# Moving loads to GpSimd's queue, building a v block on chip, storing in row pairs and doubling the output buffers, in a dilated sliding-window attention kernel with a gated output

## The chip, the cores and the metric

The kernel runs on one core of a Trainium2 chip. The metric is the device time of one execution in microseconds (us). A core has TensorE (PE in the profile; its weight loads are PEld), VectorE (DVE), ScalarE (ACT), GpSimd (POOL) and SyncE (SP), and 16 DMA engines that carry every transfer between device memory and the on-chip memory, whichever engine issued it. Each execution is given a state, fast or slow. It is slow when it took over 1.5% longer than the fastest of the same kernel.

## The reference

q, k and v have the shape (8 batches, 8 heads, 576 positions, 64). Heads 0 to 3 attend to the last 32 positions ("plain" heads). Heads 4 to 7 attend to every fourth position of the last 128 ("dilated" heads). The result x (8, 576, 512) goes through a gated unit:

```python
mask_plain = (rel >= 0) & (rel < 32)
mask_dil = (rel >= 0) & (rel < 128) & (rel % 4 == 0)
...                       # softmax, times v, heads joined to x
for k in range(5):
    gate_pre += conv_w[k] * xp[:, k:k + S, :]      # causal convolution in time
gate = 1 / (1 + exp(-gate_pre))
out = (gate * (x @ w_val)) @ w_out
```

## The kernel before

A batch has four pairs of heads: two plain, two dilated. The program walks over the 32 pairs in one hand-made order. For each pair TensorE makes scores, ScalarE the exponentials, VectorE the mask; TensorE multiplies by v, and then come the convolution, the product with w_val and, a batch later, the output tiles (w_out). In a dilated head the 576 positions are four residues of 144. The first 128 of each residue are a block of their own (vA). The last 16 of each, with the keys they need, are gathered in a second block (vB). TensorE works on two halves of the output; the second uses copies of the weights with their head halves swapped (w_val_s, w_out_s), which GpSimd makes on chip.

The parts that the change touches:

```python
out_pool = ctx.enter_context(tc.tile_pool(name="osb", bufs=4))
...
def load_v(g, a=0, e=4, eng=nc.sync):          # group g = batch, plain or dilated
    if not dil:
        for z in range(2):
            load_v_half(g, z, a, e, eng)       # plain: 64 partitions, runs of 512 bytes
    else:
        eng.dma_start(out=t["vst"][:, a:e, :], in_=v[...rows 0:512...])
        eng.dma_start(out=t["vBst"][:, a:e]..., in_=v[...rows 320:576...])
def load_group(g):                             # all on SP's queue, in this order
    k, q, remainder of k, remainder of q, then load_v(g)
def prep_v(i):                                 # GpSimd: float32 to bf16
    plain:   vP <- vPst
    dilated: vA <- vst ; vB <- vBst
def swap_out(h, m):                            # GpSimd, eight calls at pair 6
    nc.gpsimd.tensor_copy(w_out_s[D*h:D*h+D, m, :], w_st[1][D-D*h:2*D-D*h, m, :])
def out_tile(G, n):
    ...                                        # four matmuls
    osb = out_pool.tile([128, Dm], FP32, name="osb")
    nc.scalar.mul(out=osb, in_=ps, mul=0.5)
    ...
    nc.sync.dma_start(out=out[b].rearrange("(t r) n -> r t n", r=4)[r, t:t + w, :],
                      in_=osb[p:p + w, :])     # rows of one residue only
```

The softmax here doesn't subtract the row's maximum and nothing guards it: scores larger than these inputs give would overflow.

## Time and profile before

| | before |
|---|---|
| time, median of 3 (range) | 179.03 us (178.08 to 181.53) |
| span of the profiled run, state | 176.8 us, fast |
| PE busy | 159.5 us, 90% |
| bytes moved by DMA | 43.43 MB |
| longest hole of PE after 20 us | 1.33 us |

The prediction below shows and reads the main lines. The page's list of DMA queues (packets, MB, share of 16 engines' span):

```profile
q1 hardware_dynamic: 50944, 42.67, 89.1%
```

And the loads of the small remainders of q and k (qk_rest), issue to landing:

```profile
DMA to landing us min/median/max: 3.6/5.9/9.4
```

Nearly all bytes go through one queue, SP's, in packets of 42.67 MB / 50944 = 0.84 KB, and no remainder takes over 9.4 us. In this trace the transfers of that queue also land in the order of their issue: all 155 whose landing is recorded do.

### The profile page before, as it was taken

The numbers are of one execution on the slowest core, as the hardware profiler recorded it, in microseconds if no ns is written. First come the engines' busy times: TensorE is split into PE (matmuls) and PEld (weight loads), VectorE is DVE, ScalarE is ACT, GpSimd is POOL, SyncE is SP. The second block draws the span as 40 slices with busy tenths as digits, with TensorE's granted clock in tenths as the row PEclk, the third lists the DMA queues.
The fourth block names the chain that finished last, engine by engine and source line by source line (L and its number), as shares of the span: only waits on it lengthen the run. The fifth ranks groups of instructions, "written<-read, shape, count | busy, mean of one in ns | idle before, by whom it ended". The sixth has DMA issues, their size and how long they took to land.

```text
span 176.8 us, 6900 instructions
## 1 busy us (share of the span) xinstructions
PE 159.5 (90%) x2875; PEld 106.6 (60%) x2875; DVE 119.5 (68%) x299; ACT 113.8 (64%) x215; POOL 64.5 (36%) x129
## 2 busy tenths in 40 slices
PE   6798877989898899999997999789999999999990
PEld 2355544666576676677665667557677766665540
DVE  4397849773768776888695677577697869783320
ACT  3437835558777577778776777378867886654441
POOL 7673449659407610770085009300940500000000
PEclk9969999999999999999999999999999999999998
DMA  4999999999999999999999999999999322224344
GB/s 148 240 268 348 325 230 285 324 303 237 296 335 243 318 335 343 173 287 356 307 188 300 345 318 192 330 323 329 204 360 339 112 63 59 63 63 120 102 159 155
DMA packets 51528, 43.43 MB, mean 246 GB/s; under 512 B 6965, under 2 KB 45861, under 8 KB 51498
## 3 DMA queue, kind: packets, MB, share of 16 engines
q1 hardware_dynamic: 50944, 42.67, 89.1%
q8 instruction: 22, 0.36, 0.9%
q10 hardware_dynamic: 554, 0.34, 0.6%
q14 instruction: 8, 0.07, 0.1%
HBM read 33.56 MB, written 9.44 MB: 243 GB/s over the span
## 4 chain that ended last, share of the span: by engine, by line
PE 63%; DMA 21%; ACT 6%; DVE 5%; issue 2%; SPq 1%; ACTq 0%
PE ps_bank L628 16%; PE ps_bank L611 15%; PE ps_bank L594 10%; DMA out_dram<-osb 8%; PE ps_bank L378 5%; DMA qk_rest<-in_q_dram 4%; DMA k_nat<-in_k_dram 3%; DMA vPst<-in_v_dram 3%; PE ps_sc L499 3%; PE ps_sc L513 3%; PE ps_sc L449 3%; PE ps_bank L548 2%; DMA q_nat<-in_q_dram 2%; PE ps_sc L466 2%; DVE et L478 2%
## 5 line engine op out<-in xcount | busy, mean ns | idle before, releaser
L469 ACT ACTIVATE et<-ps_sc 128x576 bf16<-128x576 f32 x64 | 38.2, 649 | 13.7 <-PE ps_sc L449 9.0
L633 ACT ACTIVATE osb<-ps_bank 128x512 f32<-128x512 f32 x36 | 21.9, 609 | 28.9 <-PE ps_bank L628 18.0
L617 DVE SCALAR_TENSOR_TENSOR y<-gate,ps_bank 128x288 bf16<-128x288 bf16 x64 | 28.3, 450 | 13.0 <-PE ps_bank L611 10.6
L594 PE MATMUL ps_bank<-xT,conv_diag 64*64 64x288 bf16 (+1 forms) x768 | 27.6, 266 | 0.6 <-ACT osb L633 0.6
L529 DVE TENSOR_TENSOR xn<-ps_sc,rec 128x768 bf16<-128x768 f32 (+1 forms) x27 | 25.8, 955 | 0.9
L603 ACT ACTIVATE gate<-ps_bank 128x288 bf16<-128x288 f32 x64 | 23.1, 423 | 1.8 <-PE ps_bank L594 1.7
L478 DVE TENSOR_TENSOR et<-et,mask_d 128x576 bf16<-128x576 bf16 x32 | 15.8, 495 | 10.2 <-ACT et L469 10.2
L611 PE MATMUL ps_bank<-xT,w_val_s 128*128 128x288 bf16 x128 | 20.7, 285 | 2.1 <-issue 1.3
L193 POOL CAST k_b<-k_nat 128x512 bf16<-128x512 f32 x10 | 6.5, 681 | 42.3 <-DMA k_nat<-in_k_dram 33.1
L594 PEld LDWEIGHTS <-conv_diag 64*64 64x64 bf16 x768 | 18.9, 106 | 3.6 <-issue 1.2
L611 PE MATMUL ps_bank<-xT,w_val_b 128*128 128x288 bf16 x128 | 20.1, 286 | 0.4 <-DVE xT L563 0.4
L628 PEld LDWEIGHTS <-y 128*128 128x128 bf16 x144 | 12.6, 97 | 11.8 <-DVE y L617 0.9
L478 DVE TENSOR_TENSOR et<-et,mask_p 128x576 bf16<-128x576 bf16 x32 | 16.0, 501 | 4.8 <-ACT et L469 4.8
L202 POOL CAST vP<-vPst 128x768 bf16<-128x768 f32 x16 | 13.1, 841 | 15.6 <-DMA vPst<-in_v_dram 5.8
L628 PE MATMUL ps_bank<-w_out_s,y 128*128 128x512 bf16 x72 | 18.3, 379 | 0.1
L628 PE MATMUL ps_bank<-w_out_b,y 128*128 128x512 bf16 x72 | 18.5, 379 | 0.0
L563 DVE COPY xT<-ps_bank 128x576 bf16<-128x576 bf16 x32 | 14.6, 455 | 4.7 <-PE ps_bank L561 2.4
L611 PEld LDWEIGHTS <-w_val_s 128*128 128x128 bf16 x128 | 12.0, 97 | 6.2 <-issue 1.0
L207 POOL CAST vA<-v_st 128x512 bf16<-128x512 f32 x16 | 11.3, 705 | 10.3 <-DMA v_st<-in_v_dram 5.3
L611 PEld LDWEIGHTS <-w_val_b 128*128 128x128 bf16 x128 | 11.6, 98 | 3.7 <-issue 0.2
L393 ACT COPY kT<-ps_bank 128x1024 bf16<-128x1024 bf16 (+1 forms) x10 | 8.5, 849 | 6.1 <-PE ps_bank L370 5.9
L528 DVE RECIPROCAL rec<-ps_sc 128x12 f32<-128x12 f32 (+1 forms) x27 | 6.2, 231 | 7.7 <-PE ps_sc L499 6.7
(100 smaller groups left out, 248.4 us busy)
## 6 DMA issues: line engine op xcount, KB each, us to landing
k_nat<-in_k_dram SPq DMA_DIRECT2D x12, 512.0 KB, 6.0
q_nat<-in_q_dram SPq DMA_DIRECT2D x12, 512.0 KB, 6.9
vPst<-in_v_dram SPq DMA_DIRECT2D x12, 384.0 KB, 7.7
v_st<-in_v_dram SPq DMA_DIRECT2D x6, 512.0 KB, 5.7
k_nat<-in_k_dram SPq DMA_DIRECT2D x8, 256.0 KB, 5.9
out_dram<-osb SPq DMA_DIRECT2D x8, 256.0 KB, 6.1
q_nat<-in_q_dram SPq DMA_DIRECT2D x7, 256.0 KB, 5.8
out_dram<-osb SPq DMA_DIRECT2D x8, 224.0 KB, 5.4
```

What stands on the lines that cost most here:

```text
L202: nc.gpsimd.tensor_copy(vPs[b % NVP][:, a:e, :, 0:D], vPst[b % NVP][:, a * NB // 2:e * NB // 2, :].rearrange("p (h u) (j d) -> p h (u j) d ...
L207: nc.gpsimd.tensor_copy(vAs[b % NVD][:, a:e, :, 0:D], t["vst"][:, a:e, :].rearrange("p h (r d) -> p h r d", r=DIL))
L469: nc.scalar.activation(out=e3, in_=ps[:, :, 0:HB], func=AF.Exp, scale=scale)
L478: nc.vector.tensor_tensor(out=e3, in0=e3, in1=m, op=ALU.mult)
L529: nc.vector.tensor_tensor(out=dst, in0=av[:, :, :, 0:D], in1=rec[0:R, :, :, None].to_broadcast([R, 2, 6, D]), op=ALU.mult)
L563: nc.vector.tensor_copy(xTs[b % NXT][:, c, :, 2:], pr)
L594: nc.tensor.matmul(out=pss[G][D * hp:D * hp + D, o * T:(o + n) * T], lhsT=conv_diag[D * h:D * h + D, c, K - 1 - m, :], rhs=xt[D * h:D * h ...
L603: nc.scalar.activation(out=gate, in_=pss[G][:, 0:HB], func=AF.Tanh, scale=0.5)
L611: nc.tensor.matmul(out=ps[:, 0:HB], lhsT=w[:, mc, c * 128:(c + 1) * 128], rhs=xt[:, mc, 2 * G:2 * G + 2, 2:], start=(mc == 0), stop=(mc == ...
L617: nc.vector.scalar_tensor_tensor(out=y_half[G][:, c, b % YB * HB:(b % YB + 1) * HB], in0=gates.pop((b, c, G)), scalar=1.0, in1=ps[:, 0:HB] ...
L628: nc.tensor.matmul(out=ps, lhsT=y_half[G][:, c, y0:y0 + 128], rhs=w[:, c, :], start=(c == 0), stop=(c == NCH - 1),)
L633: nc.scalar.mul(out=osb, in_=ps, mul=0.5)
```

## The change

Its intent is to take work from the full DMA engines and from SP. It has four parts: the first rows of vB are copied on chip from vA's staging tile, so that only 64 KB per batch are loaded for it; the plain v of batches 2 to 7 and the small remainders of dilated v are issued by GpSimd instead of SP; the output rows are stored in row pairs, with 48 stores instead of 64; and there are eight output buffers instead of four. The diff, cut to its core (the constant mask and key layout for vB change with it):

```diff
-    out_pool = ctx.enter_context(tc.tile_pool(name="osb", bufs=4))
+    out_pool = ctx.enter_context(tc.tile_pool(name="osb", bufs=8))
...                                                       # load_v, dilated
-            eng.dma_start(out=t["vBst"]..., in_=v[b, 4 + a:4 + e, DIL * TB:S, :]...)
+            for w in range(2):
+                eng.dma_start(out=t["vR"][D * w + 32:D * w + 32 + TR, a:e, :], in_=...)
...                                                       # load_group
-        load_v(g)
+        if g % 2:
+            load_v(g, 0, 4, nc.gpsimd)
...                                                       # prep_v, dilated
-            nc.gpsimd.tensor_copy(vBs[...][:, a:e, :, 0:D], t["vBst"][:, a:e, :, :])
+            for w in range(2):
+                for (p0, n, src) in ((0, 32, t["vst"][96:128, ...]), (32, 16, t["vR"][...])):
+                    nc.gpsimd.tensor_copy(vBs[...][D*w+p0:D*w+p0+n, a:e, :, 0:D], src...)
...                                                       # out_tile
-                out=out[b].rearrange("(t r) n -> r t n", r=4)[r, t:t + w, :],
+                out=bass.AP(..., ap=[[DIL * Dm, w // 2], [Dm, 2], [1, Dm]]),
...                                                       # main loop
         elif i == 5:
             prep_v(7)
+            load_v(4, 0, 4, nc.gpsimd)                    # plain v of batches 2 and 3:
+            load_v(6, 0, 4, nc.gpsimd)                    # four transfers
         elif i == 6:
             ...swap_out(h, m)...                          # w_out_s
         elif i > 6:
+            if c == 0 and b + 2 < B:
+                load_v(2 * (b + 2), 0, 4, nc.gpsimd)      # batches 4 to 7: eight transfers
```

## The prediction

> **What bounds the kernel now.** I read the page's busy shares first, then the table of stretches, the chain that ended last, the list of waits, and last the timelines of single engines where a gap stood out.
>
> ```profile
> PE 159.5 (90%) x2875; PEld 106.6 (60%) x2875; DVE 119.5 (68%) x299; ACT 113.8 (64%) x215; POOL 64.5 (36%) x129
> DMA  4999999999999999999999999999999322224344
> 20.00:30.00 10.00, 7.56 (x169) 4.82 (x165) 7.18 (x21) 4.91 (x11) 6.19 (x13) 1.00 1.13 248
> 90.00:100.00 10.00, 8.69 (x151) 5.73 (x152) 6.46 (x16) 6.12 (x11) 5.11 (x9) 1.00 1.08 282
> 110.00:120.00 10.00, 8.49 (x141) 5.64 (x142) 6.42 (x16) 5.83 (x11) 1.80 (x3) 1.00 1.06 326
> 140.00:150.00 10.00, 10.00 (x204) 6.75 (x203) 7.84 (x19) 7.17 (x14) 0.00 (x0) 1.00 0.19 55
> ```
>
> The first two lines are from the page, the rest from the table of stretches (after the length: PE, weight loads, DVE, ACT, POOL, then granted clock, DMA share, GB/s). The DMA engines are full until about 137 us, yet that is not the bound for most of it: from 40 us on PE is busy 9.4 to 10 of each 10 us, and it stays so after 140 us, when the DMA share is only 0.19. The exceptions are the start (7.56 at 20 to 30 us), 90 to 100 us and 110 to 120 us. So there are two stages: a start fed by DMA, then a long stage at PE's pace with a few holes.
>
> The size of the holes follows from the chain. The same instruction (the transposes of line 378, second pair of a batch) marks the batches:
>
> ```profile
> 72.06 0.45 PE ps_bank L378 x8
> ...
> 89.68 0.45 PE ps_bank L378 x8
> ...
> 94.91 1.31 issue
> ...
> 107.40 6.62 DMA out_dram<-osb
> ...
> 129.95 0.45 PE ps_bank L378 x8
> ...
> 147.57 0.45 PE ps_bank L378 x8
> ```
>
> A batch takes 89.68 - 72.06 = 17.62 us with four output tiles, and again 147.57 - 129.95 = 17.62. The two between take 40.27. They hold one output tile more each (0.87 us of PE in the chain), so 2 x 17.62 + 2 x 0.87 = 36.98 was due, and 3.3 us are lost. The 1.31 "issue" is one part of it; the other, 2.0 us, is the store that the chain passes through:
>
> ```profile
> ACT osb L633 <- DMA out_dram<-osb: 5.7, 3, 2.8
> PE ps_bank L611 <- issue: 1.3, 1, 1.3
> ```
>
> With four output buffers, ACT's eviction waits until a store issued four tiles before has landed (here 6.6 us under full queues); ACT being in order, the exponentials behind it start late and PE with them. The first of the three such waits (1.75 us at 61.3 us) cost PE 0.56.
>
> **What the Trainium skill says.** "DMA: Bandwidth & Descriptors", section "Issuing engines are not separate DMA queues": transfers from every issuing engine share the same 16 DMA engines, so another queue saves only issue time. I therefore count nothing for bandwidth in moving plain v to GpSimd; the trace of before has no GpSimd transfer and cannot confirm it. The same page, section "SWDGE vs HWDGE vs iDMA": a transfer issued from GpSimd has its descriptors computed by the Q7 cores. So GpSimd pays for it in its own instruction stream, at a price this trace doesn't show. "GPSIMD Engine Reference", section "Specifications": each core owns 16 partitions. A copy over 16 or 32 partitions should thus cost what its length in a partition costs. The trace agrees: casts of 512 elements take 610 ns on 64 partitions (w_out_s) and 631 on 128 (w_out_b).
>
> **The change, part by part.**
>
> Second dilated v block. Before, it is read whole from memory:
>
> ```profile
> vB_st<-in_v_dram SPq DMA_DIRECT2D x6, 256.0 KB, 6.1
> vB_st<-in_v_dram SPq DMA_DIRECT2D x4, 128.0 KB, 5.2
> ```
>
> That is 2,048 KB. Now only the 16 last rows of each residue come from memory: 64 KB per batch, 512 KB in all; 1.5 MB of 43.4 MB go away. On the path this counts only in the start. There, PE waits 1.33 us for k of pair 4 (22.6 us) and then for its q. Two of these blocks are queued before it, 192 KB less; at the 330 GB/s of that stretch this is 0.6 us. The price is on GpSimd: one cast (0.40 us for 256 elements) becomes four of the same length, about 1.2 us more per pair, or, where the heads are now taken four at a time, four of 0.62 instead of two of 0.41. ACT's kB copy shrinks from 384 to 256 columns (0.53 to about 0.4 us, six times), off the path. DVE gets four memsets more of some 0.5 us, but it idles 2.38 us before its first real work at 5.73 us: nothing.
>
> Eight output buffers. A store may now land eight tiles later, some 30 us at a tile every 4.4 us, against landings of 2 to 8.5 us. All three waits should go: 2.0 us at 105 to 116 us and 0.56 us at 61 us, say 2.4 us.
>
> Row pairs. 64 stores become 48 and the bytes stay. The issues (0.42 us each) are on SP, which is off the path. DVE's line 617 writes every second element, but reads float32 from PSUM at 450 ns for 288 elements, about one element a cycle already; I count no change. PE's instructions are the same, in the same order.
>
> Plain v on GpSimd's queue. 24 transfers move there (12 plain, 12 remainders). SP loses waits and issues, off the path. But four of them, the plain v of batches 2 and 3, are put just before the swapped copy of w_out, and that copy has a deadline:
>
> ```profile
> 38.69 0.63 POOL L210 CAST vB<-vB_st 128x256 bf16<-128x256 f32 x1
> 39.38 5.24 POOL L355 CAST w_out_s<-w_st 64x512 bf16<-64x512 f32 x8
> ...
> 46.03 1.02 PE L628 MATMUL ps_bank<-w_out_s,y 128*128 128x512 bf16 x4
> ```
>
> The copy ends at 44.62 and PE reads it at 46.03: 1.4 us of slack. Afterwards pair 7's v lands some 0.9 us sooner (288 KB less in front of it), its three more casts take up to 1.2 us, and PE arrives about 0.6 us earlier. That leaves 1.4 + 0.9 - 1.2 - 0.6 = 0.5 us of slack for four issues. SP needs 0.65 us for one such transfer of plain v (1.31 for two), each of 768 runs of 512 bytes; a software generator is hardly faster. At 0.65 us the four take 2.6 and PE stalls 2.1 us; at 1 us each 3.5; at 0.3 each under 1. I choose 2.2 us, below the middle, since the small casts could overlap on different cores and the place looks chosen. A stall here is paid in full, for PE has no idle time left afterwards.
>
> Dilated v in batch 2. The vB cast ended at 56.5 us and PE needed it at 58.76. Behind the same cast of k it now ends after 1.0 + 4 x 0.62 = 3.5 us instead of 1.0; 0.3 us may be lost. Later batches had 3.7 us of slack or more.
>
> The "issue" hole of 1.31 us stands where nothing visible waited. If it is an instruction fetch delayed by full DMA queues, fewer bytes may remove it: I take half, 0.65.
>
> Sum: -0.6 - 2.4 - 0.65 + 2.2 + 0.3 = -1.15 us. From the median of 179.0 that is about 177.8; I shade it to 177.5 because the stall is the least certain term and the only large one against the change.
>
> **The rivals.** (1) GpSimd takes the place of the store wait: issues of 1.5 us and more push the swapped weights 5 us or more past PE's need, and the time becomes 180 to 182. For it: 1.4 us of slack, and an in-order engine. Against it: GpSimd is busy only 36%, and the issue cost is unknown. (2) Issues are almost free, and the smaller load of the queues removes the 1.31 us hole too: -0.6 - 2.4 - 1.3 makes 174.7. For it: the plain 3.3 us in the chain. (3) Full queues: GpSimd's ring gets its turns on the same engines, so q and k land later and the start gains nothing, while stores have their buffers: about 177. Against it: the total of bytes falls. (4) All of it hidden: PE's work is unchanged, its idle time from 46 us to 172 us is only about 4.8 us, so more than 6 us of gain, start included, is not there.
>
> **Range and chances.** The two ends are rivals 2 and 1: 174.0 to 181.0 should hold it 8 times in 10. Faster by over 2% means below 175.4, which needs nearly the whole of the gains and a stall under half a microsecond: 0.23. Slower by over 2% means above 182.6, which needs issues near 2 us: 0.06. The rest, 0.71, lies within 2%.
>
> **What would show it.** In the changed kernel's waits, ACT's eviction should not wait for stores any more, and the batches should come every 17.6 us, or 18.5 with five tiles. In GpSimd's timeline the swapped copy should start 2 to 4 us after the last vB cast of pair 7, and PE should show an idle stretch of about 2 us before the first tile of the swapped weights, near 46 us. k of pair 4 should arrive about 0.6 us earlier. The prediction is wrong if GpSimd's issues cost well under 0.4 or over 1.5 us, if DVE's strided write is slower than 450 ns, or if new waits for v on GpSimd's queue appear in later batches.

## The result, and the profile after

The changed kernel took 189.73 us (median of four, 187.53 to 191.85; the kernel before, now with four runs, 180.28 in the same rounds). A ratio here is the mean time of one kernel's fast runs over that of the other's of the same rounds, so it isn't quite the ratio of the medians. It was 1.0515, 95% interval 1.0444 to 1.0586: slower. The changed kernel was run once more as an experiment ("after2" below, on another chip): 187.99 us, ratio 1.037 (1.0287 to 1.0452). The loss is 4 to 5%.

The first profile after fell in the slow state (span 190.1), so I read the second, which is fast (span 185.6). The page of the second, busy shares, DMA slices and queues:

```profile
PE 161.3 (87%) x2875; PEld 107.5 (58%) x2875; DVE 123.0 (66%) x301; ACT 113.8 (61%) x215; POOL 93.0 (50%) x166
DMA  5997999789999999999999999979487122122244
...
q1 hardware_dynamic: 37408, 35.98, 67.1%
q0 software_dynamic: 1728, 5.11, 12.9%
```

PE's busy time is 1.8 us longer (161.3 against 159.5 us), so 7.0 of the 8.8 us of span are idle time of PE. GpSimd's own queue has appeared (q0), and its packets are of another size: 5.11 MB / 1728 = 2.96 KB against 35.98 MB / 37408 = 0.96 KB on SP's queue. In engine time a packet of q0 takes 12.9% x 16 x 185.6 / 1728 = 0.22 us, one of q1 0.053 us.

The table of stretches of the same run (columns as in the prediction):

```profile
20.00:30.00 10.00, 6.87 (x130) 4.49 (x123) 4.73 (x14) 4.80 (x10) 5.75 (x12) 0.83 1.14 261
44.00:56.00 12.00, 8.31 (x162) 4.99 (x162) 4.15 (x11) 8.21 (x16) 8.64 (x13) 1.00 1.09 253
90.00:100.00 10.00, 8.52 (x180) 5.77 (x177) 7.21 (x16) 6.70 (x14) 7.88 (x11) 1.00 1.04 244
110.00:120.00 10.00, 8.26 (x176) 5.55 (x175) 6.70 (x15) 6.21 (x12) 5.32 (x9) 1.00 1.02 305
```

The stretch from 44 to 56 us, where the kernel before has PE busy for 11.42 of the 12 us, now has 8.31. GpSimd's and PE's timelines show what happens there and later (start, us, engine, line, operation; in brackets the idle time before it and what ended it):

```profile
42.78 3.00 POOL L156 DMA_DIRECT2D vPst<-in_v_dram  x4
45.83 5.48 POOL L360 CAST w_out_s<-w_st 64x512 bf16<-64x512 f32 x8
54.27 1.46 POOL L209 CAST vP<-vPst 128x1536 bf16<-128x1536 f32 x1 [2.96 <-DMA vPst<-in_v_dram]
60.27 1.17 POOL L197 CAST k_b<-k_nat 128x512 bf16<-128x512 f32 x2 [2.06 <-DMA k_nat<-in_k_dram]
```

```profile
50.03 0.38 PE L633 MATMUL ps_bank<-w_out_s,y 128*128 128x512 bf16 x1 [0.95 <-POOL w_out_s L360]
51.36 0.38 PE L633 MATMUL ps_bank<-w_out_s,y 128*128 128x512 bf16 x1 [0.95 <-POOL w_out_s L360]
55.79 0.55 PE L501 MATMUL ps_sc<-vP,et 64*128 64x65 bf16 x24 [0.96 <-POOL vP L209]
...
97.93 0.20 PE L451 MATMUL ps_sc<-qT,kT 64*64 64x96 bf16 x1 [1.48 <-issue]
114.16 0.78 PE L596 MATMUL ps_bank<-xT,conv_diag 64*64 64x288 bf16 x21 [1.74 <-issue]
```

An issue costs GpSimd 0.75 us (four in 3.00). The eight copies of w_out_s come behind them and PE waits for them. GpSimd itself then idles for v and for k. Later PE stops twice for "issue", that is, for nothing that the profile shows. The loads on SP's queue explain the late k. The landing times of the remainders, then two of their issues in SP's timeline:

```profile
DMA to landing us min/median/max: 3.8/6.6/19.6
```

```profile
45.03 6.01 SPq L136 DMA_DIRECT2D qk_rest<-in_k_dram  x1
51.10 0.62 SPq L136 DMA_DIRECT2D qk_rest<-in_q_dram  x1
```

The longest landing is 19.6 us (9.4 before; 22.4 in the slow profile). SP was held for 6.01 us in the first issue, where the next takes 0.62. k itself took up to 16.6 us (8.4 before).

One part of the prediction came true in the main. ScalarE's evictions waited for a store twice, for 1.0 us in all, instead of three times and 5.7 us. Their list of waits is now headed by a wait for PE, which is a consequence, not a cause:

```profile
ACT osb L638 <- PE ps_bank L633: 26.8, 25, 3.5
```

### The profile page after: what moved, and what is told of

It is laid out like the page before. It is cut to its first block, busy times and chain, and to the rows that moved or that the text cites. A ratio compares the mean times of both kernels' runs of the same rounds, so it can differ in the third digit from the quotient of the medians.

```text
span 190.1 us, 6884 instructions
## 1 busy us (share of the span) xinstructions
PE 166.1 (87%) x2875; PEld 109.6 (58%) x2875; DVE 124.3 (65%) x301; ACT 113.9 (60%) x215; POOL 93.4 (49%) x166
## 2 busy tenths in 40 slices
DMA packets 39722, 41.87 MB, mean 220 GB/s; under 512 B 6870, under 2 KB 32710, under 8 KB 39691
## 3 DMA queue, kind: packets, MB, share of 16 engines
q1 hardware_dynamic: 37408, 35.98, 65.3%
q0 software_dynamic: 1728, 5.11, 12.3%
## 4 chain that ended last, share of the span: by engine, by line
PE 60%; DMA 26%; SPq 4%; DVE 4%; issue 2%; ACT 1%; ACTq 0%
PE ps_bank L633 17%; PE ps_bank L613 13%; DMA qk_rest<-in_k_dram 12%; DMA q_nat<-in_q_dram 11%; PE ps_bank L596 9%; PE ps_bank L383 4%; DMA vPst<-in_v_dram 4%; PE ps_sc L501 3%; PE ps_sc L468 3%; PE ps_sc L515 2%; PE ps_sc L451 2%; DVE et L480 2%; PE ps_bank L550 2%; PE ps_bank L563 1%; DVE xT L565 1%
## 5 line engine op out<-in xcount | busy, mean ns | idle before, releaser
L620 DVE SCALAR_TENSOR_TENSOR y<-gate,ps_bank 128x288 bf16<-128x288 bf16 x64 | 29.9, 476 | 13.3 <-PE ps_bank L613 11.2
L596 PE MATMUL ps_bank<-xT,conv_diag 64*64 64x288 bf16 (+1 forms) x768 | 28.5, 274 | 0.6 <-issue 0.6
L596 PEld LDWEIGHTS <-conv_diag 64*64 64x64 bf16 x768 | 19.5, 110 | 6.5 <-issue 4.0
L480 DVE TENSOR_TENSOR et<-et,mask_p 128x576 bf16<-128x576 bf16 x32 | 17.4, 544 | 8.0 <-ACT et L471 7.9
L633 PE MATMUL ps_bank<-w_out_s,y 128*128 128x512 bf16 x72 | 20.0, 397 | 2.8 <-POOL w_out_s L360 2.8
L480 DVE TENSOR_TENSOR et<-et,mask_d 128x576 bf16<-128x576 bf16 x32 | 17.1, 534 | 7.7 <-ACT et L471 7.7
L633 PEld LDWEIGHTS <-y 128*128 128x128 bf16 x144 | 12.9, 99 | 14.7 <-issue 4.1
L613 PE MATMUL ps_bank<-xT,w_val_b 128*128 128x288 bf16 x128 | 20.6, 291 | 0.4 <-DVE xT L565 0.4
L209 POOL CAST vP<-vPst 128x1536 bf16<-128x1536 f32 (+1 forms) x10 | 12.2, 1216 | 8.1 <-DMA vPst<-in_v_dram 5.2
L613 PEld LDWEIGHTS <-w_val_b 128*128 128x128 bf16 x128 | 11.8, 100 | 4.0 <-issue 0.6
L214 POOL CAST vA<-v_st 128x1024 bf16<-128x1024 f32 (+1 forms) x10 | 9.7, 965 | 8.0 <-DMA v_st<-in_v_dram 6.8
L222 POOL CAST vB<-v_rest 16x512 bf16<-16x512 f32 (+1 forms) x20 | 11.6, 581 | 1.5 <-DMA v_rest<-in_v_dram 0.5
```

The source lines that it names most:

```text
L209: nc.gpsimd.tensor_copy(vPs[b % NVP][:, a:e, :, 0:D], vPst[b % NVP][:, a * NB // 2:e * NB // 2, :].rearrange("p (h u) (j d) -> p h (u j) d ...
L222: nc.gpsimd.tensor_copy(vBs[b % NVD][D * w + p0:D * w + p0 + n, a:e, :, 0:D], src.rearrange("p h (j d) -> p h j d", j=2))
L480: nc.vector.tensor_tensor(out=e3, in0=e3, in1=m, op=ALU.mult)
L596: nc.tensor.matmul(out=pss[G][D * hp:D * hp + D, o * T:(o + n) * T], lhsT=conv_diag[D * h:D * h + D, c, K - 1 - m, :], rhs=xt[D * h:D * h ...
L613: nc.tensor.matmul(out=ps[:, 0:HB], lhsT=w[:, mc, c * 128:(c + 1) * 128], rhs=xt[:, mc, 2 * G:2 * G + 2, 2:], start=(mc == 0), stop=(mc == ...
L620: nc.vector.scalar_tensor_tensor(out=y_half[G][:, c, b % YB * HB:(b % YB + 1) * HB].rearrange("p (t r) -> p r t", r=2), in0=gates.pop((b, ...
```

## The experiments

All eighteen runs gave correct results. To compare them I added up every idle time in PE's timeline after 20 us by what ended it (us). This is a sum over the bracketed numbers of the timeline:

| run | state, span | ACT | DVE | DMA | POOL | issue | sum |
|---|---|---|---|---|---|---|---|
| before | fast 176.8 | 3.7 | 2.3 | 1.3 | 0 | 1.3 | 8.6 |
| p1_osb8 | fast 176.3 | 1.3 | 1.9 | 2.7 | 0 | 1.0 | 7.0 |
| b1_osb8_rows | fast 175.8 | 1.1 | 1.7 | 3.2 | 0 | 0.4 | 6.4 |
| a3_vSP | fast 177.3 | 1.9 | 2.5 | 3.3 | 0 | 0.5 | 8.2 |
| d2_pool | fast 182.7 | 1.3 | 2.0 | 6.1 | 0 | 0.8 | 10.2 |
| c2_first | fast 182.7 | 1.2 | 2.8 | 3.4 | 3.6 | 0.2 | 11.2 |
| a2_swapfirst | fast 187.3 | 1.2 | 2.7 | 3.5 | 7.7 | 2.2 | 17.2 |
| a8_swapDVE | fast 188.3 | 2.0 | 6.0 | 3.5 | 1.6 | 4.3 | 17.5 |
| after2 (the changed kernel) | fast 185.6 | 1.4 | 2.5 | 3.6 | 3.9 | 4.6 | 16.1 |

### First: each part alone

**p1_osb8**, the kernel before with eight output buffers only.

```diff
-    out_pool = ctx.enter_context(tc.tile_pool(name="osb", bufs=4))
+    out_pool = ctx.enter_context(tc.tile_pool(name="osb", bufs=8))
```

> The kernel before with eight output buffers and nothing else. My theory: the three waits of ACT's eviction for a landed store (5.7 us of ACT) go, and with them 2.0 + 0.56 us of PE's holes: 2 to 3 us faster, ratio 0.983 to 0.989. Rival: the wait only moves to another place (stores then sit longer in the full queues in front of loads), ratio 0.995 to 1.005.

Measured: 177.93 us median, ratio 0.9878 (0.9753 to 1.0002). No eviction waits for a store, and PE has no hole of 0.5 us or more after 58 us. This part does what was meant.

**p2_rows**, the kernel before with the row pairs only (the two hunks of `val` and `out_tile`).

```diff
-            out=y_half[G][:, c, b % YB * HB:(b % YB + 1) * HB], in0=gates.pop((b, c, G)), ...
+            out=y_half[G][...].rearrange("p (t r) -> p r t", r=2), ...     # in0 and in1 likewise
...
-                out=out[b].rearrange("(t r) n -> r t n", r=4)[r, t:t + w, :],
+                out=bass.AP(..., ap=[[DIL * Dm, w // 2], [Dm, 2], [1, Dm]]),
```

> The kernel before with products stored in row pairs (48 stores in place of 64, DVE writes every second element) and nothing else. My theory: within 0.5% of before, and DVE's line for y at about 450 to 480 ns. Rival: the strided write slows DVE enough to show (y above 550 ns, ratio above 1.01); other rival: fewer stores free places among the transfers in flight, ratio below 0.99.

Measured: 179.57 us, ratio 0.9986 (0.9901 to 1.0071). VectorE's line for y takes 477 ns instead of 450, as expected. Fewer stores alone are worth nothing that these runs can see.

**p3_vB**, the kernel before with the on-chip vB only; every load stays on SP, plain v at its old place.

```diff
-            eng.dma_start(out=t["vBst"]..., in_=v[b, 4 + a:4 + e, DIL * TB:S, :]...)
+            for w in range(2):
+                eng.dma_start(out=t["vR"][...], in_=...)                    # eng is nc.sync
...
-            nc.gpsimd.tensor_copy(vBs[...], t["vBst"][...])
+            ...four copies from t["vst"] and t["vR"], and the keys and mask of vB
```

> The kernel before with the second dilated v block copied on chip and nothing else; its remainders are loaded on SP's queue. Theory of places: at most eight transfers of the hardware queues are in flight (each waits for the one eight before it), so two small loads in place of one large one starve the DMA engines in the start: pair 4's first k transposes 0.7 to 1.5 us later than before's 22.6 us, pair 6's scores 2 us or more later than before's 36.5 us, whole ratio 1.01 to 1.025. Theory of bytes (my prediction): the start is 0.6 us earlier, ratio 0.995 to 1.0.

Measured: 182.58 us median beside 182.86 for the kernel before on the same chip, which ran in both states there. Only one of its four runs was fast (179.30), so there is no ratio, and its profile is slow. Inconclusive, but no large loss. The first k transposes of pair 4 start at 22.25 us in that profile (22.61 before), which gives the theory of places no support.

**p4_plain**, the kernel before with the plain v of batches 2 to 7 on GpSimd's queue only.

```diff
-        load_v(g)
+        if g % 2:
+            load_v(g)
...
+            load_v(4, 0, 4, nc.gpsimd)            # pair 5, before swap_out
+            load_v(6, 0, 4, nc.gpsimd)
...
+            if c == 0 and b + 2 < B:
+                load_v(2 * (b + 2), 0, 4, nc.gpsimd)
```

> The kernel before with plain v of batches 2 to 7 on GpSimd's queue and nothing else. Theory of turns: GpSimd's packets are some 3 KB against 1 KB and less on SP's queue, so while they run SP's queue gets a small share; together with the late swapped copy of w_out (PE stalls of about 3 us near 46 us) the ratio is 1.02 to 1.04, and a transfer of k or q rest issued after 40 us takes over 10 us to land. Rival, the swapped copy alone: a stall of about 3 us, landings as before, ratio 1.01 to 1.017.

Measured: 186.08 us median (182.56 to 190.36), again one fast run, so no ratio; its fastest run is 3.7 us above the fastest of the kernel before on that chip (182.56 against 178.88). In its (slow) profile a k landed after 20.0 us and a q after 17.8. The bytes are exactly those of before; only the issuing engine changed. The suspicion falls on this part.

### Second: the changed kernel, with one thing undone

**a3_vSP**, the changed kernel with every v load, the small remainders too, back on SP's queue at the old places.

```diff
-        if g % 2:
-            load_v(g, 0, 4, nc.gpsimd)
+        load_v(g)
...                                  # and the three load_v calls of the main loop removed
```

> The changed kernel with every load of v on SP's queue in the places of the kernel before, so that only GpSimd's queue is undone (on-chip copy, row pairs, eight buffers and the merged casts stay). Theory of turns: all of the loss goes and the gain of the buffers is left, ratio 0.98 to 0.99, no landing of k, q or their rest over 11 us after 40 us, no half clock after 40 us. Rival, the four small casts and the on-chip copy carry a good part of the loss: ratio 1.005 or more.

Measured: 181.31 us median, ratio 0.9953 (0.9794 to 1.0112). No landing over 9.4 us. The stretches that were hollow in the changed kernel are full again:

```profile
44.00:56.00 12.00, 10.66 (x226) 7.00 (x226) 6.68 (x17) 8.98 (x18) 5.54 (x8) 1.00 1.14 287
...
110.00:120.00 10.00, 10.00 (x188) 6.90 (x188) 8.07 (x22) 7.24 (x13) 4.96 (x6) 1.00 1.09 299
```

This is the cleanest pair for the accounting: a3_vSP and after2 differ only in the queue and place of the v loads (and ran on two chips), and both profiles are fast. The idle sums are 8.2 and 16.1, a difference of 7.9 us of the 8.3 us between the spans. By kind: GpSimd's results 3.9 more, "issue" 4.1 more, direct waits for DMA only 0.3 more.

**a7_plainSP**, the changed kernel with only the plain v back on SP; the remainders of dilated v stay on GpSimd's queue.

```diff
-        if g % 2:
-            load_v(g, 0, 4, nc.gpsimd)
+        load_v(g, 0, 4, nc.gpsimd if g % 2 else nc.sync)
...                                  # and the three load_v calls of the main loop removed
```

> The changed kernel with plain v back on SP's queue, the small remainders of dilated v still on GpSimd's. Theory of turns: 64 KB a batch is too little to starve anything: ratio 0.98 to 0.995. Rival, each issue on GpSimd costs (about 0.5 us each, and they stand in front of casts): ratio 1.0 to 1.02.

Measured: 180.22 us, ratio 0.9881 (0.9746 to 1.0016). So the twelve small transfers on GpSimd's queue do no harm that these runs can see; the twelve large ones do.

**a2_swapfirst**, the changed kernel with the eight copies of w_out_s ahead of the four loads.

```diff
         elif i == 5:
             prep_v(7)
-            load_v(4, 0, 4, nc.gpsimd)
-            load_v(6, 0, 4, nc.gpsimd)
         elif i == 6:
             ...swap_out(h, m)...
+            load_v(4, 0, 4, nc.gpsimd)
+            load_v(6, 0, 4, nc.gpsimd)
```

> The changed kernel with the four loads of plain v for batches 2 and 3 put behind the swapped copy of w_out on GpSimd instead of in front of it. Theory of the late copy (the one my prediction named): PE's wait for w_out_s (2.8 us) and the half clock after it go and little else was wrong: ratio to before about 1.00 to 1.02. Theory of turns (GpSimd's large packets starve SP's queue whenever they run): the wait for w_out_s goes, but k or q rest issued beside those loads still takes over 10 us to land and PE still waits 2 us or more near 60 to 72 us: ratio 1.02 to 1.045.

Measured: 191.1 us, ratio 1.0436 (1.0293 to 1.0579). PE no longer waits for w_out_s, but now for v of the next batch, whose load starts some 4 us later (47.06 us, 42.78 in after2). So one late result was swapped for another, and this run can't say whether the late copy was the loss; c1_late below can:

```profile
60.54 0.84 PE L501 MATMUL ps_sc<-vP,et 64*128 64x65 bf16 x24 [7.67 <-POOL vP L209]
```

**a5_spread**, as a2_swapfirst, with batch 3's plain v issued three pairs later still.

```diff
             ...swap_out(h, m)...
             load_v(4, 0, 4, nc.gpsimd)
-            load_v(6, 0, 4, nc.gpsimd)
         elif i > 6:
+            if i == 9:
+                load_v(6, 0, 4, nc.gpsimd)
```

> The changed kernel with the swapped copy first and plain v of batch 3 loaded three pairs later than batch 2's, so that at most two of the 384 KB loads of GpSimd's queue run at once. Theory of turns with the burst as the cause: landings of k and rest beside them fall to about 8 to 11 us, the hole near 65 us shrinks below 1 us, ratio 0.99 to 1.015. If every load of GpSimd's queue hurts however few run at once: as the kernel with only the order mended, 1.02 to 1.045.

Measured: 190.99 us, ratio 1.056 (1.0446 to 1.0675); slow profile. The same wait for vP is 8.17 us. My theory of a burst (four loads at once) is not tested by it, because this delay hides everything else. What both runs show is that on GpSimd's in-order stream the loads and the copies of w_out_s both have a deadline, and there isn't room for both.

**a8_swapDVE**, the changed kernel with the copies of w_out_s on VectorE.

```diff
-        nc.gpsimd.tensor_copy(
+        nc.vector.tensor_copy(
             w_out_s[D * h:D * h + D, m, :], ...)
```

> The changed kernel with the eight swap copies of w_out on VectorE in place of GpSimd: TensorE's wait for w_out_s (2.84 us in the profile after) should be under 0.5, and the plain v loads are issued where the changed kernel issues them, so vP is not late as it was in the run with the swap first. Theory 1 (turns): qk_rest or k_nat still lands after 14 to 24 us, the holes for vB, qk_rest and the instruction fetch stay, and the time is 184 to 188 (1.02 to 1.04), 2 to 5 under the changed kernel. Theory 2 (late copy): 178 to 181.

Measured: 190.1 us, ratio 1.0501 (1.0426 to 1.0575); fast profile. The wait for w_out_s is gone, but VectorE's masks come late instead:

```profile
43.23 0.30 PE L515 MATMUL ps_sc<-vA,et 128*128 128x65 bf16 x4 [3.62 <-DVE et L480]
```

So this run, too, swapped one late copy for another. It doesn't measure the loss without the late copy; I expected 184 to 188. It does show that landings of 18.3 us (k) and 19.3 us (remainders), and 4.3 us of "issue", stay when GpSimd doesn't make these copies.

### Third: the queue by itself

Loads that nobody waits for separate the queue from the copies. **d_pool** and **d_sp** are the kernel before plus four loads of plain v (1.05 MB) into an unused tile, issued behind the copies of w_out_s on GpSimd, or at the same place of the program on SP.

```diff
                     swap_out(h, m)
+            for bb in (2, 3):
+                for z in range(2):
+                    nc.gpsimd.dma_start(          # d_sp: nc.sync.dma_start
+                        out=dum[bb - 2][D * z:D * z + D, :, :], in_=...plain v of batch bb...)
```

> The kernel before, unchanged, plus four more loads (1.05 MB of plain v, the same shapes as in the change) into a tile that nobody reads, issued on GpSimd's queue after the on-chip swap copy of w_out, so no instruction waits for them and no copy on GpSimd comes later than before except those behind 3 us of issue time. Theory of turns (GpSimd's packets of about 3 KB alternate with SP's of about 1 KB on the same 16 engines): k, q or the remainders of q and k that are under way at that time land late, the longest of them after 12 to 18 us instead of 9.4, a hole of 1 to 3 us opens on TensorE between 58 and 70 us, the clock falls to a half for 3.4 us after it, and the time is 183 to 187 (1.5 to 4% over the kernel before in the same rounds). Rival (the loss of the change came from GpSimd's copies being made later, w_out_s and vP, and not from the queue): all landings stay under 10.5 us and the time within 1%.

> As d_pool, with the same four extra loads issued on SP's queue, behind the k and q loads of group 6. Both carry 1.05 MB more than before, some 3.2 us of all 16 engines at 330 GB/s. Theory of turns: on SP's own queue the extra loads stand behind the loads of k and q and can't take turns from them, so k_nat and qk_rest land within 10.5 us and the time is within 1% of before. Rival (any extra bytes in that stretch do it, whatever the queue): as slow as d_pool, within 1% of it.

Measured: d_pool 185.67 us, ratio 1.0284 (1.022 to 1.0348); d_sp 188.08 us, ratio 1.0308 (1.0209 to 1.0407). The landings came out as the theory of turns has it (at most: k 13.5 and q 14.0 us with GpSimd; 9.4 and 10.2 with SP), but the times are the same, which is what the rival expected. The profiles tell why. In both, PE's longest hole is a wait for ScalarE's eviction: 3.18 us in d_pool, 5.18 in d_sp (slow profile). With four output buffers any extra load delays a store and with it ScalarE. The changed kernel has eight, so this pair answers another question.

**d2_pool** and **d2_sp** repeat it on the kernel with eight output buffers and row pairs. The unused tile is then the staging tile of w_val, dead by that time.

```diff
                     swap_out(h, m)
+            dum = w_st[0]...                      # as 16 runs of 128 numbers
+            for (bb, j0, n) in ((2, 0, 12), (3, 12, 4)):
+                for z in range(2):
+                    nc.gpsimd.dma_start(          # d2_sp: nc.sync.dma_start
+                        out=dum[D * z:D * z + D, j0:j0 + n, :], in_=...plain v of batch bb...)
```

> The kernel with eight output buffers and row pairs (0.979 of the kernel before), plus four extra loads of 1.05 MB that nobody waits for, on GpSimd's queue behind the swap copy. Theory 1 (turns): k_nat or q_nat lands after 12 to 18 us as in d_pool (13.5 and 14.0), and TensorE has a hole of 1 to 3 us for it between 55 and 75 us, perhaps a half clock after it: 1.00 to 1.03 of the kernel before. Theory 3 (bytes): the same time as d2_sp within 0.7%. If the landings are late and no hole comes of it (0.975 to 0.99), late landings of this size are hidden while the other loads are not on GpSimd, and the loss of the changed kernel needs the late copies as well.

> As d2_pool with the four extra loads on SP's queue. Theory 1: landings of k_nat, q_nat and qk_rest within 10.5 us as in d_sp; the stores queue behind the extra loads, but with eight buffers ScalarE has no wait for them: 0.975 to 0.995 of the kernel before. Theory 3: as slow as d2_pool, both over 1.00.

Measured: d2_pool 184.49 us, ratio 1.0203 (1.0146 to 1.0261); d2_sp 179.40 us, ratio 0.988 (0.9798 to 0.9962). The same bytes at the same place of the program cost some 6 us more on GpSimd's queue than on SP's (mean of the fast runs 184.6 and 178.8), where they cost little or nothing (the kernel without them is at 0.9791, see below). The stretch after GpSimd's issues, in the table of stretches of d2_pool:

```profile
52.00:58.00 6.00, 1.89 (x9) 1.23 (x10) 1.84 (x5) 0.41 (x1) 0.00 (x0) 0.80 1.08 245
```

the same in that of d2_sp:

```profile
52.00:58.00 6.00, 6.00 (x105) 3.82 (x102) 3.68 (x9) 3.37 (x7) 1.33 (x3) 0.72 0.97 271
```

and PE's timeline in d2_pool:

```profile
53.98 0.23 PE L413 MATMUL ps_bank<-ident,qk_rest 128*128 128x128 bf16 x1 [2.22 <-DMA qk_rest<-in_k_dram]
56.34 0.29 PE L413 MATMUL ps_bank<-ident,qk_rest 128*128 128x128 bf16 x1 [2.13 <-DMA qk_rest<-in_q_dram]
```

The load of q that was issued between 44 and 54 us, in the list of DMA issues (KB, us to landing), first in d2_pool, then in d2_sp:

```profile
q_nat<-in_q_dram SPq DMA_DIRECT2D x1, 512.0 KB, 13.6
```

```profile
q_nat<-in_q_dram SPq DMA_DIRECT2D x1, 512.0 KB, 8.1
```

With the DMA engines about full in both (share 1.08 and 0.97; 245 and 271 GB/s), PE is busy for 1.89 of 6 us in one and all 6 in the other. But the same place of the program was not the same time: GpSimd issued the four loads from 44.8 to 47.8 us, SP only from 56.3 to 62.6, behind the k, q and v that stand before them in its order. So in d2_sp the extra bytes were not yet on the way in nearly all of this stretch. The pair shows what it costs when they pass the loads that are wanted first. It doesn't separate turns and packet size from that: a run with the same bytes ahead of k and q on SP's own queue was not made. The profile of d2_sp is a slow one, with two "issue" holes of 2.0 and 2.2 us at other places, yet it has no late landing. (The 0.80 and 0.72 in the two rows of stretches are the granted clock, of which more below.)

That the two queues do take turns can be seen in d2_pool. The list of DMA queues for 52 to 54 us alone (packets, MB, share of 16 engines):

```profile
q0 software_dynamic: 94, 0.34, 78.7%
q1 hardware_dynamic: 96, 0.09, 26.8%
```

One packet of SP's goes with one of GpSimd's, and SP's queue is left with a quarter of the engines, though k and q wait on it.

**x1_act**, the changed kernel with the plain v issued by ScalarE (`nc.scalar` for `nc.gpsimd` in the three calls), a second hardware queue with small packets.

```diff
-            load_v(4, 0, 4, nc.gpsimd)
-            load_v(6, 0, 4, nc.gpsimd)
+            load_v(4, 0, 4, nc.scalar)
+            load_v(6, 0, 4, nc.scalar)
...
-                load_v(2 * (b + 2), 0, 4, nc.gpsimd)
+                load_v(2 * (b + 2), 0, 4, nc.scalar)
```

> The changed kernel with its plain v loads issued by ScalarE, on its hardware queue, in place of GpSimd, at the same places of the program; the small v remainders stay on GpSimd. Theory of turns with the packet size as its lever: ScalarE's packets are as small as SP's, so the two queues share the engines about evenly instead of 3 to 1; w_out_s is no longer late (GpSimd issues nothing there); the longest landing of qk_rest is 9 to 13 us instead of 22.4 and the time 180 to 184, unless ScalarE itself is held up by the issue (then its copies come late, and the wait of TensorE is for ACT). Rival 1 (any second queue beside SP's starves it alike): landings of 15 to 22 us and 186 or more. Rival 2 (only GpSimd's own time matters): as before, 178 to 181.

Measured: 192.95 us, ratio 1.0691 (1.0619 to 1.0764). The landings are as expected for a queue with small packets: k at most 11.2, q 11.8, remainders 9.4 us, beside 16.6, 12.6 and 19.6 in after2. The time is worse for the reason allowed for in the expectation: ScalarE, which has real work, was held by its own issues. ScalarE's timeline, then PE's behind it:

```profile
36.90 5.54 ACTq L156 DMA_DIRECT2D vPst<-in_v_dram  x3
```

```profile
43.88 0.46 PE L501 MATMUL ps_sc<-vP,et 64*128 64x65 bf16 x10 [10.29 <-ACT et L471]
```

### Fourth: which loads

**c1_late**: the first four large loads back on SP, the later eight on GpSimd. **c2_first**: the reverse.

```diff
         if g % 2:                                 # load_group, c1_late:
+        if g % 2 or g in (4, 6):                  #   (c2_first: g % 2 or g > 6)
-            load_v(g, 0, 4, nc.gpsimd)
+            load_v(g, 0, 4, nc.gpsimd if g % 2 else nc.sync)
...                                                # and the calls for those groups removed
```

> The changed kernel with the plain v of batches 2 and 3 (the first four loads, 1.57 MB) issued by SP with their groups as before, and only the later eight on GpSimd. If the loss is made in the one stretch where the four loads meet the loads of groups 5 and 6: no wait for w_out_s, no hole over 1 us between 44 and 75 us, 0.985 to 1.00 of the kernel before. If every load on GpSimd costs its share (8 of 12): 1.02 to 1.035, with holes of 2 us behind the later loads.

> The changed kernel with only the first four plain v loads (batches 2 and 3) on GpSimd's queue; the later eight go to SP with their groups. If the loss adds up over the loads, this is what c1_late's 1.035 leaves of 1.050: 1.010 to 1.025, 182 to 186, with TensorE's wait for w_out_s (2 to 3 us) and late k_nat or qk_rest (over 12 us) between 48 and 72 us, and no landing over 10.5 us after that. If the parts don't add (each alone starts the same loss): 1.03 to 1.05.

Measured: c1_late 190.15 us, ratio 1.0352 (1.0258 to 1.0447), slow profile; c2_first 185.38 us, where the two fast runs (184.41 and 183.44) give 183.9 / 181.2 = 1.015 without an interval. I had hoped for c1_late to be free; it isn't. It has no late w_out_s and still loses 3.5%, so the theory that the late copy is the whole loss falls here. Both sets of loads cost, and the later eight seem to cost more. They cost in different ways. In the table c2_first has all of the waits for GpSimd (3.6 of the 3.9 us) and no "issue" holes (0.2); c1_late's slow profile has 6.7 us of "issue" and no wait for GpSimd.

**after2**, the changed kernel again and unaltered, for a fast profile.

> The changed kernel itself, unaltered. If the profile in the slow state told the truth of the waits, the fast one (span 185 to 187) shows w_out_s late by 2 to 3 us between 47 and 54 us, qk_rest or k_nat landing after 14 us or more, and holes for vB and qk_rest; the holes of instruction fetch and the number of half clocks may differ by one or two, which is worth 2 to 5 us. 1.045 to 1.06 of the kernel before.

Measured as told above. The wait for w_out_s was 2.3 us in all (2.84 in the slow profile). Only one half-clock stretch, near 25 us, is left, where the slow profile had four.

### The best of the parts

**b1_osb8_rows**: the kernel before with eight output buffers and the row pairs; no load moved (the edits of p1_osb8 and p2_rows together).

> The kernel before with the two parts of the change that cost nothing on any engine: eight output buffers and the products stored in row pairs. Every v load stays where it was. Theory: ScalarE's waits for stores are gone as in the run with eight buffers alone (ratio 0.988), the rows add nothing (0.9986), so 0.980 to 0.993 of the kernel before, and no hole of TensorE over 2 us after 58 us. Rival (the gain of eight buffers alone was scatter of the runs): 0.995 to 1.005.

Measured: 178.48 us median of six, ratio 0.9791 (0.9699 to 0.9883). Only two of the six runs are fast (175.62 and 177.70), and the ratio rests on them. Its page:

```profile
PE 160.1 (91%) x2850; PEld 107.7 (61%) x2875; DVE 121.7 (69%) x299; ACT 114.2 (65%) x215; POOL 64.1 (36%) x129
```

This version is faster than both the kernel before and the changed kernel. Whether the on-chip vB would add to it stays open: a3_vSP, which has it as well, is at 0.9953, and the two intervals overlap.

## Why the prediction was wrong

The prediction was 177.5 us in 174 to 181; 189.7 and 188.0 were measured. Its steps:

- **"I therefore count nothing for bandwidth in moving plain v to GpSimd."** This is the step that failed: it took the move to be free for the loads that stay on SP's queue. The sum of bandwidth doesn't seem to change (q0 takes 12.9% of the 16 engines' span in after2, and so does ScalarE's queue in x1_act, with packets of 0.51 KB), but the order of service does. In the Trainium skill, "DMA: Bandwidth & Descriptors", section "Queues, rings and completion order", says that each DMA engine goes round-robin between queues "at packet granularity". I quoted the neighbouring section and didn't look this one up. The trace agrees: 94 packets to 96 in the two us shown above. On SP's queue a large load that is issued late stands behind the k and q that are wanted first. On GpSimd's queue it takes every second turn, with packets that hold an engine 0.22 us against 0.053. As an estimate from these, while both queues are full SP gets 0.053 / (0.053 + 0.22) = about a fifth of the engines; measured was 27% from 52 to 54 us in d2_pool, and about half in the two us before and after. An estimate for d2_pool: its extra loads are 320 packets (45 to 60 us); in 44 to 54 us a packet of that queue takes 37.7% x 16 x 10 / 212 = 0.285 us, so SP stands back 320 x 0.285 / 16 = 5.7 us. Measured: q landed after 13.6 us with them and after 8.1 in d2_sp, where they came behind it, 5.5 later. The pair d2 shows the effect on the time: 1.020 against 0.988. That the delay is as long as the extra bytes' own time also fits a rival: any 1.05 MB put ahead of q would delay it so, turns or not. That packet size is the lever is supported by x1_act's landings, not shown: no run changes the packet size alone on one queue. In the changed kernel the step costs 7.9 us of PE's idle time (after2 against a3_vSP), of which the wait for w_out_s, the only part that I had counted, is 2.3.
- **"SP loses waits and issues, off the path."** SP lost issues, but was held 6.01 us in one of them. The next load in its order, the remainder of q, was issued at 51.10 and landed 15.6 us later, and PE had a hole of 0.65 us for it at 66.7 us.
- **The stall for w_out_s, +2.2 us.** Right in place and size: an issue costs 0.75 us (inside the 0.3 to 1 us that I allowed), and PE lost 2.3 us (2.84 in the slow profile). It is the loss in its visible place, less than a third of the whole.
- **vB in batch 2, +0.3 us.** It was 0.33 us in after2, as predicted, and 0.32 more in batch 3; 2.04 in the slow profile, 1.3 in c2_first, and 0 in a3_vSP, which has the same casts. So the casts alone are not the cause; GpSimd waits for a late k first and makes vB after it. (a7_plainSP's slow profile has 1.4 with only the remainders on GpSimd's queue; its k landed after 10.3 us.) With vP, late for the same queue (0.96 us), this makes up the rest of the 3.9 us.
- **The "issue" hole, -0.65 us.** Right without the move (1.3 us before; 1.0, 0.4 and 0.5 in p1_osb8, b1_osb8_rows and a3_vSP), and of the wrong sign with it: 4.6 in after2. Fast profiles with the later large loads on GpSimd's queue have 2.2 to 4.6 us. Those without have at most 1.3, except d_pool with 3.0; and d2_sp's slow profile has 5.2 with nothing on GpSimd's queue. I took these holes for instruction fetches, which go through the same DMA engines: the profile's page lists a queue of kind "instruction", q8, with 22 packets per run. The traces bear that out. In the profiles of all runs 29 "issue" holes of 0.5 us or more lie after 20 us, and each ends 1.3 to 1.8 us after a packet of q8 has landed, though these come some 7 us apart. In after2 the holes lie 768, 512 and 512 of PE's matmuls and weight loads apart, where a packet serves 262 (5767 in 22). So PE stands still there for its next instructions. That these fetches are late because they too wait for turns is inferred; nothing here shows it, and the 4 us of "issue" are the part of the loss whose last cause stays open. The prediction hoped for fewer bytes; the bytes fell from 43.43 to 41.87 MB, and the holes grew.
- **The output buffers, -2.4 us.** Right in size: 0.988 alone is about 2.2 us of 180, though its interval just reaches 1. **Row pairs, nothing:** right, though VectorE's line for y takes 477 ns, which the prediction had named as a sign of being wrong.
- **The start, -0.6 us.** Not settled. In after2 the first k of pair 4 came 0.58 us earlier than before (22.03 against 22.61), and PE then waited 2.09 us for q. In the slow profile it came 0.75 later. The starts scatter this much among kernels with the same early code.

The third rival of the prediction came nearest to the mechanism ("GpSimd's ring gets its turns on the same engines, so q and k land later") and was wrong in its size: I let it cost the 0.6 us gained at the start, because I thought of the start and not of 45 to 70 us, where the same turns delay what PE needs next. "The total of bytes falls", which I held against it, is no argument about order.

The last piece is the clock. After some holes PE gets half of its clock for a while, and such a hole is then paid twice. In the table of stretches of d2_pool (2 us each; the third number from the right is the granted clock):

```profile
54.00:56.00 2.00, 0.21 (x1) 0.07 (x1) 0.00 (x0) 0.00 (x0) 0.00 (x0) 0.90 1.08 232
...
58.00:60.00 2.00, 2.00 (x51) 1.40 (x49) 0.92 (x3) 1.02 (x2) 0.00 (x0) 0.50 1.11 338
60.00:62.00 2.00, 2.00 (x26) 1.61 (x17) 1.12 (x3) 0.97 (x4) 1.24 (x3) 0.50 1.21 234
```

Summed over the stretch from 54 to 64 us the missing clock is 3.4 us. That is enough to explain why d2_pool's span is 6.9 us longer than b1_osb8_rows' with only 3.8 us more idle time. The Trainium skill describes this in "TensorE: Matmul & The Clock Gate", "Part 1: The HAM clock gate": half rate after an idle window of about 3.4 us. The trace agrees with the halving; on the length of the hole it differs (see the last section). In the fast profile of the changed kernel this adds nothing against a3_vSP: each has one such stretch near 25 us, and a3_vSP's is the longer (mean clock from 20 to 30 us 0.66 against 0.83). In the slow profile there are four, 6.8 us in all, and that may be part of what makes its runs scatter.

## What to carry to other kernels

Moving these loads to another queue freed no bandwidth that the runs show, but it gave up the order of one queue: a large transfer that would have waited behind the urgent ones then takes turns with them, and with larger packets it can take most of the time (78.7% against 26.8% here). Before moving one, look in the profile at bytes per packet of both queues and ask what will be in flight on the old queue at that moment, and what on the new issuing engine stands behind the issue. To test such a suspicion, add a load that nobody waits for, once on each queue, and make sure first that the test kernel has no other wait, such as scarce output buffers, that answers in its place. Look also at when each queue really issued the load: here the same place of the program was 44.8 us on one and 56.3 us on the other.

## What the Trainium skill lacked or had wrong

- "DMA: Bandwidth & Descriptors", section "Issuing engines are not separate DMA queues", says that issuing from several engines only saves the issue time. It doesn't say that it can cost: 1.020 against 0.988 for the same 1.05 MB on GpSimd's and on SP's queue, at the same place of the program. A sentence there on unequal packets (here 2.96 KB, 0.22 us of an engine, beside 0.96 KB, 0.053 us) might have changed this prediction.
- The same page, section "Anatomy of one DMA", calls descriptor generation on the GpSimd path "small, variable". Here one load of 768 runs of 512 bytes held GpSimd 0.75 us, and one of the small remainders 0.52 us.
- The same page doesn't say how long an issue on a hardware queue can hold its engine when the queue is backed up: 6.01 us on SP, 5.54 us for three on ScalarE.
- "TensorE: Matmul & The Clock Gate" puts the idle time that halves the clock at about 3.4 us. Here single holes of 2.0 us (d2_sp, a slow profile, at 51.3 us) and 2.1 us (after2, at 24.5 us) were followed by it, and ones of 1.74, 1.79 and 2.16 us (after2, a8_swapDVE and a2_swapfirst) were not. So the length of one hole doesn't decide it. Two holes of 0.95 us within 2 us were followed by it in c2_first and not in after2.
- No page says by how much PE can stand still for its instruction fetches when the DMA engines are full; it would belong to "Runtime: NRT & Kernel Launch". The "issue" holes were 0.2 to 1.3 us in most fast profiles and up to 4.6 in others.
